# Linear attention with decay feeding an MLP: another layout for the first queries, the key decay moved into v, a mask read with step zero, and another planner

## Chip, cores and metric

The kernel runs on one core of one Trainium2 chip. The metric is device time in microseconds (us) of one execution, as a median over several runs; lower is better. TensorE (PE) multiplies, VectorE (DVE), ScalarE (ACT) and GpSimd (POOL) work elementwise, SyncE (SP) only issues DMAs.

## The reference

Attention with a per-head decay `lam` over blocks of 64 tokens (4 batches, 8 heads, 768 tokens, head size 64), and then an MLP whose activation is h + sin(alpha h)^2 / alpha.

```python
def _attn_ref(q, k, v, lam):
    Dmask = np.where(rel >= 0, lam[:, None, None] ** rel[None], 0.0)
    for b in range(nb):
        intra = np.einsum('bhic,bhjc->bhij', qb, kb) * Dmask[None]
        intra = np.einsum('bhij,bhjd->bhid', intra, vb)
        inter = np.einsum('bhid,bhde->bhie', qb * lam_pow[None], kv_state)
        out[:, :, sl] = intra + inter
        kv_state = lam_block * kv_state + np.einsum('bhsd,bhse->bhde', kb * rev_pow[None], vb)

def _moe_ref(x, w_in, w_out, alpha):          # x: 3072 x 512
    h = x @ w_in                              # 512 x 2048
    s = np.sin(alpha * h)
    return (h + s * s / (alpha + 1e-09)) @ w_out
```

The block size does not change the result; the kernel works in blocks of 128 tokens.

## The kernel before

**Attention.** There are 24 blocks of 128 tokens (6 for each batch), numbered `s`. The decay lam^(i-j) is split into lam^i on the query side and lam^-j on the key side, so that no pair needs its own factor: `Lq` and `Lk` hold the powers, made by iota, a multiply by ln(lam) (`lnL`, DVE), and two exponentials (ACT). For each block, `scale_block` multiplies q by Lq (L464, POOL, two instructions for a pair of blocks) and k by Lk (L471, DVE for blocks 0 and 1, else POOL) into `qk2`, and casts v to bf16 (L473, ACT, or POOL for late blocks). q is loaded for two blocks at once, with two neighbouring tokens on a partition, so that a row of a transfer has 512 bytes; rows of k and v have 256 bytes. `piece_Q` and `piece_T` transpose q and k on PE (L506, L488) and copy them to `qkT` (L511, L493); from block 12 on a DMA transpose does it (L479, on SP's queue). `part_S` multiplies keys by queries into two PSUM banks (L543), and DVE multiplies 128 x 1024 values by `mask` into `Sm` (L552). `part_Z` adds k^T v to the running state in PSUM (L568) and copies it (`Zc`, `Zd`). `part_O` multiplies the state by q (L616, L603) and v by Sm (L623) and copies the output to `xT`, which is the transposed input of the MLP (L632).

**MLP.** Tokens go in six chunks of 512. An A unit makes 128 hidden features of a chunk: four matmuls of 512 columns (L671), a sine (ACT L681), a square (POOL L686 or ACT L685) and h + u/alpha on DVE (L688) into `gT`. `unit_A2` does the same for two feature groups on half a chunk (L705, L715, L719 or L720, L723), so that a chunk can start before all its tokens are there; it serves chunk 1 and the beginnings of chunks 0 and 2. A B unit adds four products with w2 (L736) into a bank for the output; after the fourth, ACT copies it (L749) and a DMA stores it.

**Weights.** The first quarter of w1 comes through SP into `ws` and is cast by DVE (L391). The other three quarters and the four of w2 come through POOL's queue, which casts on the way.

**Order.** Every operation is recorded with an engine (or a choice of engines with durations), its reads and its writes. `_Plan` then plays the program with these durations and appends, one at a time, the operation that can start first; within a margin PE and SP take the one recorded first (less `lead`). SP keeps the order recorded, PE may look 40 operations ahead, ACT, DVE and POOL take what is ready. The order found is the order of each engine's queue, and each wait becomes a semaphore. `_transfers` estimates when loads land, and the planner is run again with that.

**Filler.** While PE has nothing to do before the first A unit, the planner puts `spin` into the holes: matmuls of 512 columns whose result is not used (L829). `P.filler` names what they read.

Of the kernel before, what the change touches and what calls it, by code (L numbers as in the profile page):

```python
# [13 lines left out]
class _Op:  # L14


    def __init__(self, eng, emit, dur, reads, writes, dma, after, issue, lat, runs=64):
        self.eng, self.emit, self.dur = eng, emit, dur
        self.given = eng
        self.issue, self.lat, self.runs = issue, lat, runs  # L20
        self.lead = 0
        self.reads, self.writes, self.dma = reads, writes, dma
        self.port = False
        self.after = after
        self.deps = set()
        self.needed = False
        self.count = None
        self.start = None
        self.done = None
        self.knows = None  # L30


class _Plan:

    AHEAD = {"PE": 40, "SP": 1}
    SLACK = 0.3  # L40
    EARLY = 0.0, 0.0

    LAT = 0.2
# [10 lines left out]
    def op(self, eng, emit, dur, reads=(), writes=(), dma=None, after=(), issue=0.4, lat=2.6, runs=64):  # L54
# [14 lines left out]
        o.deps.discard(o)  # L69
        o.lead = self.lead  # L70
# [4 lines left out]
    def _transfers(order):  # L75
# [5 lines left out]
        left = {e: [[o.start + 0.8, o.runs, o.dur / o.runs, o] for o in sorted(q, key=lambda o: o.start)]  # L81
# [19 lines left out]
    def _settle(self):  # L101

        filler, lands, best = self.filler, {}, None
        for _ in range(8):
            self.filler = filler
            for o in self.ops:
                o.eng, o.start, o.done = o.given, None, None
            order = self._order(lands)
            new = self._transfers(order)
            off = sum(abs(t - o.done) for o, t in new.items())  # L110
            state = [(o, o.eng, o.start, o.done) for o in order]
            if best is None or off < best[0]:
                best = off, order, state
            lands = new
# [4 lines left out]
    def _order(self, lands):  # L119
        index = {o: i - o.lead for i, o in enumerate(self.ops)}  # L120
        left = {}
        for o in self.ops:
            left.setdefault(o.eng if isinstance(o.eng, str) else "any", []).append(o)
        fixed = {e: left.pop(e, []) for e in ("PE", "SP")}
        free = [o for e in left for o in left[e]]
        clock = {e: 0.8 for e in ("PE", "SP", "ACT", "DVE", "POOL")}
        wire = 0.0
        port = 0.0
        order = []

        def ready(o):
            t = 0.0
            for d in o.deps:
                if d.done is None:
                    return None
                t = max(t, d.done + (0.0 if d.eng == o.eng else self.LAT))
            return t

        while fixed["PE"] or fixed["SP"] or free:
            best = None  # L140
            for e in ("PE", "SP"):
                can = []
                for o in fixed[e][:self.AHEAD[e]]:
                    r = ready(o)
                    if r is not None:
                        can.append((max(r, clock[e]), index[o], o, e, o.dur))
                if can:
                    soon = min(c[0] for c in can)
                    soon += self.EARLY[1] if e == "PE" and soon < self.EARLY[0] else self.SLACK
                    c = min((c for c in can if c[0] <= soon), key=lambda c: c[1])  # L150
                    if best is None or c[:2] < best[:2]:
                        best = c
            for o in free:
                r = ready(o)
                if r is None:
                    continue
                if o.port:
                    r = max(r, port)
                if isinstance(o.eng, str):
                    c = (max(r, clock[o.eng]), index[o], o, o.eng, o.dur)  # L160
                else:
                    _, e, d = min((max(r, clock[e]) + d + late, e, d) for e, d, late in o.eng)
                    c = (max(r, clock[e]), index[o], o, e, d)
                if best is None or c[:2] < best[:2]:
                    best = c
            t, _, o, e, dur = best
            if e == "PE" and self.filler is not None:
                emit, reads, last = self.filler
                if last.start is not None:
                    self.filler = None  # L170
                else:
                    deps = [self.writer[b] for b in reads]
                    at = max([clock["PE"]] + [d.done + self.LAT if d.done is not None else t for d in deps])
                    n = int((t - at) / 0.4)
                    if n > 0:
                        f = _Op("PE", lambda h, n=n: emit(h, n), 0.4 * n, tuple(reads), (), None, (), 0, 0)
                        f.deps = set(deps)
                        f.start, f.done = at, at + 0.4 * n
                        order.append(f)
            if isinstance(o.eng, str):  # L180
                (fixed[e] if e in fixed else free).remove(o)
            else:
                free.remove(o)
                o.eng = e
            o.start = t
            if o.dma is not None:
                clock[e] = t + o.issue
                wire = max(wire, t + 0.8) + dur
                o.done = max(t + 0.8 + o.dur + o.lat, lands[o]) if o in lands else wire + o.lat
            else:  # L190
                clock[e] = o.done = t + dur
                if o.port and e != "ACT":
                    port = o.done
            order.append(o)
        return order
# [48 lines left out]
def bass_lightning_attn__then__act_snake_kernel(  # L244
# [14 lines left out]
    BL = 128  # L259
# [17 lines left out]
    RU = 4  # L277

    es = contextlib.ExitStack()
    with es:  # L280
# [18 lines left out]
        q32 = ring("q32", RL // 2, [128, H, 2, D], F32)  # L299
# [8 lines left out]
        mask = sb("mask", [128, 8, 128], BF16)  # L308
        maskf = sb("maskf", [128, 128], F32)
# [4 lines left out]
        E_i = sb("E_i", [128, 2 * NB, H], I32)  # L314
        E_f = sb("E_f", [128, 2 * NB, H], F32)
        lnL = sb("lnL", [128, 2 * NB, H], F32)
        Lq = sb("Lq", [128, NB, H], F32)
# [12 lines left out]
        def _(_unused_eng):  # L330
# [5 lines left out]
            P.EARLY = 20.0, 0.3  # L336
# [4 lines left out]
            def load(dst, src, key, dur, sem, eng="SP", lat=2.6, after=(), issue=0.4, runs=64):  # L341
# [3 lines left out]
            def load_q(s, after=()):  # L345
# [3 lines left out]
                for lo, hi in ((0, 4), (4, H)) if s < 4 else ((0, H),):  # L349
                    last["q32", s] = load(  # L350
                        q32[j][:, lo:hi, :, :].rearrange("p h t d -> p h (t d)"),
                        q[b, lo:hi, n * BL:(n + 2) * BL, :].rearrange("h (p t) d -> p h (t d)", t=2),
                        [("q32", j, a) for a in range(lo // 4, hi // 4)],
                        (0.9 if s == 0 else 1.1 if s < 4 else 2.3), f"q32{j}" + (str(lo) if s < 4 else ""),
                        lat=2.7, after=after, runs=8 * (hi - lo),
                    )

            def load_kv(s, which="kv"):
                b, n, j = s // NB, s % NB, s % RL
                for nm, src, dst in (("k32", k, k32), ("v32", v, v32)):  # L360
                    if nm[0] in which:
# [3 lines left out]
                            (nm, j), 1.1, f"{nm}{j}", lat=2.7,  # L365
# [7 lines left out]
            def load_w1(i, after):  # L373
# [3 lines left out]
                    [("w1", 2 * i), ("w1", 2 * i + 1)], 2.55, f"w1{i}", "POOL", 3.8, after, 0.8, 32,  # L377
                )

            def load_w1_first():  # L380
                for lo in (0, 256):
# [3 lines left out]
                        ("ws", lo), 1.65, f"ws{lo}", lat=2.7, runs=32,  # L385
# [8 lines left out]
            def load_w2(i, after):  # L394
# [3 lines left out]
                    [("w2", 2 * i), ("w2", 2 * i + 1)], 2.55, f"w2{i}", "POOL", 3.8, after, 0.8, 32,  # L398
# [3 lines left out]
            load(lam_bc[:, :], bass.AP(lam.tensor, 0, [[0, 128], [1, H]]), "lam", 0.1, "lam", "ACT", runs=1)  # L402
# [527 lines left out]
```

## Time and profile before

| what | value |
|---|---|
| median of 3 runs | 222.93 us (222.86 to 223.31) |
| profiled execution | 223.52 us, of which the span of the trace is 221.4 |
| PE busy | 208.6 us, 94% of the span, 1645 matmuls |
| ACT, DVE, POOL busy | 155.9, 122.6, 89.1 us |
| first matmul of the MLP | 19.89 us |
| HBM read, written | 27.28 MB, 6.29 MB |
| under 512 bytes | 63520 of 83651 DMA packets |

Times in the trace count from the start of the span. Busy time of PE is the time in which a matmul is in flight, the pipelined overlap counted once. A line number such as L543 is that of the kernel before. A wait is put down to the engine and line whose semaphore came last.

### The profile page before, as it was taken

To read this page: it belongs to the slowest core of one execution; us is meant where nothing else is said; L and a number is where in the kernel's file an instruction comes from. 1 tells how busy PE (TensorE), PEld (TensorE's weight loads), DVE (VectorE), ACT (ScalarE), POOL (GpSimd) and SP (SyncE) were. 2 spreads that over 40 slices of the span, in tenths; PEclk is the share of its full clock that TensorE was granted. 3 is DMA by queue.
4 is the path that set the end of the run, shared out by engine and by line. 5 is a ranking of instruction groups with operands and counts; after the bars stand their busy time and mean duration, and the time that the engine had idled before them with its cause. 6 is when DMAs were issued, how large, how long until landed. Compare 5 with 4: busy or idle time off the path is not lost.

```text
span 221.4 us, 4062 instructions
## 1 busy us (share of the span) xinstructions
PE 208.6 (94%) x1645; PEld 110.7 (50%) x1645; DVE 122.6 (55%) x184; ACT 155.9 (70%) x277; POOL 89.1 (40%) x100
## 2 busy tenths in 40 slices
PE   3889987899898999999999999999999999999995
PEld 1446433456575785545445444545545444444444
DVE  4687775354777887667655455645465544445100
ACT  3735994347697997788788887877788677778211
POOL 4386763454978776863576103011001011110100
DMA  5999999999999999999999752110110011101112
GB/s 131 236 232 271 206 214 208 217 235 237 233 245 275 242 191 245 219 254 189 276 240 245 155 112 33 47 50 0 47 50 21 26 47 50 47 0 49 75 70 95
DMA packets 83651, 33.31 MB, mean 150 GB/s; under 512 B 63520, under 2 KB 80688, under 8 KB 83632
## 3 DMA queue, kind: packets, MB, share of 16 engines
q1 hardware_dynamic: 76880, 24.25, 53.6%
q0 software_dynamic: 3696, 3.67, 9.9%
q10 hardware_dynamic: 3056, 5.13, 6.4%
q8 instruction: 13, 0.21, 0.4%
q14 instruction: 6, 0.05, 0.1%
HBM read 27.28 MB, written 6.29 MB: 152 GB/s over the span
## 4 chain that ended last, share of the span: by engine, by line
PE 63%; DMA 24%; POOL 4%; SPq 4%; ACT 2%; DVE 1%; issue 1%
PE bank L736 32%; PE bank L671 24%; DMA k<-in_k_dram 10%; DMA q<-in_q_dram 5%; DMA v<-in_v_dram 4%; DMA w<-in_moe_w_in_dram 4%; SPq L342 4%; PE bank L705 3%; PE bank L623 2%; PE bank L543 2%; POOL qk L471 1%; POOL qk L464 1%; PE bank L603 1%; POOL u L720 1%; DVE gT L723 1%
## 5 line engine op out<-in xcount | busy, mean ns | idle before, releaser
L736 PE MATMUL bank<-w,gT 128*128 128x512 bf16 (+1 forms) x400 | 94.8, 371 | 0.0
L688 DVE SCALAR_TENSOR_TENSOR gT<-u,rinv,bank 128x512 bf16<-128x512 bf16 x74 | 54.6, 746 | 51.7 <-ACT u L685 34.2
L671 PE MATMUL bank<-xT,w 128*128 128x512 bf16 x296 | 74.2, 379 | 0.6 <-DVE gT L688 0.6
L681 ACT ACTIVATE t<-bank,alpha 128x512 bf16<-128x512 f32 x74 | 50.6, 686 | 24.1 <-PE bank L671 24.0
L736 PEld LDWEIGHTS bank<-w,gT 128*128 128x128 bf16 x400 | 37.7, 98 | 39.6
L686 POOL TENSOR_TENSOR u<-t 128x512 bf16<-128x512 bf16 x19 | 19.7, 1040 | 80.7 <-ACT t L681 79.7
L671 PEld LDWEIGHTS bank<-xT,w 128*128 128x128 bf16 x296 | 28.5, 98 | 34.9 <-DVE gT L688 1.1
L685 ACT ACTIVATE u<-t 128x512 bf16<-128x512 bf16 x55 | 34.4, 629 | 1.8 <-DVE gT L723 0.3
L552 DVE TENSOR_TENSOR Sm<-bank,mask 128x1024 bf16<-128x1024 f32 x24 | 29.2, 1222 | 10.3 <-PE bank L568 7.7
L464 POOL TENSOR_TENSOR qk<-q,Lq 128x512 bf16<-128x512 f32 x24 | 24.5, 1044 | 21.7 <-DMA q<-in_q_dram 18.1
L471 POOL TENSOR_TENSOR qk<-k,Lk 128x512 bf16<-128x512 f32 x22 | 22.9, 1044 | 7.2 <-DMA k<-in_k_dram 7.0
L749 ACT COPY osb<-bank 128x512 f32<-128x512 f32 (+1 forms) x25 | 14.2, 569 | 14.8 <-PE bank L736 14.8
L705 PE MATMUL bank<-xT,w 128*128 128x256 bf16 x176 | 22.3, 273 | 2.0 <-DVE gT L723 2.0
L723 DVE SCALAR_TENSOR_TENSOR gT<-u,rinv,bank 128x256 bf16<-128x256 bf16 x44 | 19.1, 476 | 7.2 <-POOL u L720 4.1
L715 ACT ACTIVATE t<-bank,alpha 128x256 bf16<-128x256 f32 x44 | 18.5, 471 | 3.3 <-PE bank L705 3.1
L705 PEld LDWEIGHTS bank<-xT,w 128*128 128x128 bf16 x176 | 16.2, 98 | 5.5 <-DVE gT L723 3.0
L473 ACT CAST v<-v 128x512 bf16<-128x512 f32 x18 | 11.0, 615 | 7.6 <-DMA v<-in_v_dram 7.6
L632 ACT CAST xT<-bank 128x512 bf16<-128x512 f32 (+1 forms) x18 | 12.9, 716 | 2.8 <-PE bank L568 1.6
L720 POOL TENSOR_TENSOR u<-t 128x512 bf16<-128x512 bf16 x11 | 11.3, 1039 | 4.7 <-ACT t L715 4.6
L543 PE MATMUL bank<-qkT 64*128 64x128 bf16 x192 | 9.8, 226 | 0.2 <-DVE qkT L493 0.2
L623 PE MATMUL bank<-Sm,v 128*64 128x128 bf16 x192 | 9.9, 225 | 0.0
L829 PE MATMUL bank<-mask,ident 128*128 128x512 bf16 x12 | 5.7, 564 | 3.7 <-DVE mask L429 3.7
(55 smaller groups left out, 111.4 us busy)
## 6 DMA issues: line engine op xcount, KB each, us to landing
k<-in_k_dram SPq DMA_DIRECT2D x24, 256.0 KB, 5.5
v<-in_v_dram SPq DMA_DIRECT2D x24, 256.0 KB, 5.5
q<-in_q_dram SPq DMA_DIRECT2D x10, 512.0 KB, 5.5
out_dram<-osb ACTq DMA_DIRECT2D x19, 256.0 KB, 2.0
w<-in_moe_w_out_dram POOLq DMA_DIRECT2D x4, 512.0 KB, 13.1
w<-in_moe_w_in_dram POOLq DMA_DIRECT2D x3, 512.0 KB, 9.0
q<-in_q_dram SPq DMA_DIRECT2D x4, 256.0 KB, 4.6
ws<-in_moe_w_in_dram SPq DMA_DIRECT2D x2, 512.0 KB, 5.4
```

Source lines behind the costliest of these rows:

```text
L464: lambda e, a=a: e.tensor_tensor(qk2[:, j:j + 2, 4 * a:4 * a + 4, :], q32[jq][:, 4 * a:4 * a + 4, :, :].rearrange("p h t d -> p t h d"), b ...
L471: lambda e: e.tensor_tensor(qk2[:, j, H:2 * H, :], k32[jl][:, :, :], lk, ALU.mult), 0.7 if s in (0,1) else 1.05,
L552: op("DVE", lambda e: e.tensor_tensor(Sm[s % 2][:, :, :], banks[:, 512 * b0:512 * b0 + 1024].rearrange("p (c i) -> p c i", i=128), mask[:, ...
L671: ins = e.matmul(ps[hb][:, c0:c1], w1[:, kc, 128 * m:128 * (m + 1)], xT[x][:, kc, c0:c1], start=(kc == 0 and c0 == lo), stop=(kc == NKC - ...
L681: op("ACT", lambda e: e.activation(t16[ju][:, w], ps[hb][:, w], ACTF.Sin, scale=alpha[:, m:m + 1]), 0.69 * f, [bank(hb), "alpha"], [("t16" ...
L685: lambda e: (e.activation(u16[ju][:, w], t16[ju][:, w], ACTF.Square) if e is nc.scalar else e.tensor_tensor(u16[ju][:, w], t16[ju][:, w], ...
L686: e.tensor_tensor(u16[ju][:, w], t16[ju][:, w], t16[ju][:, w], ALU.mult)), 0,
L688: op("DVE", lambda e: e.scalar_tensor_tensor(out=gT[g][:, m, w], in0=u16[ju][:, w], scalar=rinv[:, m:m + 1], in1=ps[hb][:, w], op0=ALU.mul ...
L705: ins = e.matmul(ps[hb][:, 256 * i:256 * i + 256], w1[:, kc, 128 * (m + i):128 * (m + i + 1)], xT[x][:, kc, lo:lo + 256], start=(kc == 0 a ...
L715: op("ACT", lambda e, i=i: e.activation(t16[ju][:, 256 * i:256 * i + 256], ps[hb][:, 256 * i:256 * i + 256], ACTF.Sin, scale=alpha[:, m + ...
L723: op("DVE", lambda e, i=i: e.scalar_tensor_tensor(out=gT[g][:, m + i, lo:lo + 256], in0=u16[ju][:, 256 * i:256 * i + 256], scalar=rinv[:, ...
L736: ins = e.matmul(ps[ob][:, w], gT[g][:, m, 128 * s4:128 * (s4 + 1)], w2[:, m, w], start=(m == 0), stop=(m == NM - 1),)
```

## The change

Five things are changed.

1. **q of blocks 0 to 3** is loaded by two DMAs, each with four heads, all 512 tokens and four neighbouring tokens on a partition (rows of 1,024 bytes), before any k or v. Their scaling has its own powers (`Lq4`, a third iota and a third exponential) and is split between POOL and DVE. Since a column of the transposed q now stands for every fourth token, `part_S` and `part_O` of these blocks read 32 columns out of each of four tiles of `qkT`, and so need all four, and the mask of these blocks is another one.
2. **The decay of the keys** is multiplied into v (POOL) and k is only cast (ACT, or ACT or POOL from block 12 on). The products k v and S v are the same.
3. **The mask** is kept once for each layout (128 x 128) and read with a step of zero over the eight heads.
4. **The planner** models start-up, hand-over and pipelining of engines and the start of transfers, gives margins to all engines, and takes other durations. Early weight loads on POOL wait for v of block 2 instead of k of block 3, and the first of them is given priority.
5. **The filler** reads `Zd` in place of `mask`, which is no longer wide enough.

```diff
-                for lo, hi in ((0, 4), (4, H)) if s < 4 else ((0, H),):
+                if s < 4:
+                    for a in range(2):
+                        last["q32", s] = load(
+                            q32[:, a, :, :, :].rearrange("p (h x) t d -> p h (x t d)", x=2),
+                            q[0, 4 * a:4 * a + 4, 0:4 * BL, :].rearrange("h (p t) d -> p h (t d)", t=4),
+                            [("q32", a, 0), ("q32", a, 1)], 1.45, f"q32{a}", lat=1.25, after=after, runs=32,
+                        )
+                    return
...
-                ported(op("DVE" if s in (0,1) else "POOL",
-                   lambda e: e.tensor_tensor(qk2[:, j, H:2 * H, :], k32[jl][:, :, :], lk, ALU.mult), ...
-                op((("ACT", 0.62, 0.0), ("POOL", 1.05, 0.3)) if s > 11 else "ACT", ... v2[j] from v32[jl]
+                op((("ACT", 0.62, 0.0), ("POOL", 0.62, 0.3)) if s > 11 else "ACT", ... qk2[:, j, H:2 * H] from k32[jl]
+                ported(op("POOL",
+                   lambda e: e.tensor_tensor(v2[j][:, :, :], v32[jl][:, :, :], lk, ALU.mult), 1.05,
...
-                                qkT[r, jt, 4 + jp, :], qkT[r, jq:jq + 2, jp, u],
+                                qkT[r, jt, 4 + jp, :], qkT[r, jq:jq + nq, jp, u],
...
-                        mask[:, :, :], ALU.mult), 1.25, [bank(b0), bank(b1), "mask"], [("Sm", s % 2)])
+                        bass.AP(mask[s >= 4], 0, [[128, 128], [0, 8], [1, 128]]), ALU.mult), 1.22, ...
...
             piece_Q(0, 4)
+            piece_Q(2, 6)
             piece_T(0, 3)
...
-            piece_Q(2, 4)
...
             for i in range(1, 4):
-                load_w1(i, [last["k32", 3]])
+                P.lead = 400 if i <= 1 else 0
+                load_w1(i, [last["v32", 2]])
...
-                    ins = e.matmul(ps[0][:, :], ident[:, :], mask[:, 0:4, :].rearrange("p a b -> p (a b)"))
+                    ins = e.matmul(ps[0][:, :], ident[:, :], Zd[0][:, :, :].rearrange("p a b -> p (a b)"))
...
-                    P.filler = (spin, ("mask", "ident"), u)
+                    P.filler = (spin, (("Zd", 0, 0), ("Zd", 0, 1), "ident"), u)
```

Of the planner, the new constants, the choice of the next operation, and the lines that place the filler (the last four are as before but for names and the hand-over time):

```diff
-    AHEAD = {"PE": 40, "SP": 1}
-    SLACK = 0.3
-    LAT = 0.2
+    AHEAD = 40
+    WINDOW = {"PE": 0.3, "ACT": 0.1, "DVE": 0.1, "POOL": 0.1}
+    PIPE = {"ACT": 0.11, "DVE": 0.09, "POOL": 0.045, "PE": 0.0}
+    HOP = {"PE": 0.055, "ACT": 0.035, "DVE": 0.035, "POOL": 0.075, "SP": 0.1}
+    DRAIN = 0.085
+    MOVES = ()
...
+                soon = min(x[0] for x in c) + self.WINDOW.get(e, 0.0)
+                x = min((x for x in c if x[0] <= soon), key=lambda x: x[1])
+                if best is None or x[0] < best[0]:
+                    best = x[0], x[2], e, x[3]
...
+                    deps = [self.writer[b] for b in reads]
+                    free = max([clock["PE"]] + [d.done + self.HOP["PE"] if d.done is not None else t for d in deps])
+                    n = int((t - free) / 0.4)
+                    if n > 0:
```

More of the change, by code (lines that the diff above doesn't have):

```diff
@@ L52, in __init__, with op @@
         self.lead = 0
-    def op(self, eng, emit, dur, reads=(), writes=(), dma=None, after=(), issue=0.4, lat=2.6, runs=64):
+    def op(self, eng, emit, dur, reads=(), writes=(), dma=None, after=(), issue=0.55, lat=1.4, runs=64, lag=None):
         o = _Op(eng, emit, dur, tuple(reads), tuple(writes), dma, after, issue, lat, runs)
@@ L69, in op @@
         o.deps.discard(o)
+        if lag is not None:
+            o.lag = lag
         o.lead = self.lead
@@ L101, in _settle @@
     def _settle(self):
[L103 to L111, printed above, removed]
+        prio = {o: i - o.lead for i, o in enumerate(self.ops)}
+        for at, width, kind, by in self.MOVES:
+            for o in self.ops[at:at + width]:
+                if kind == "all" or o.given == kind or (kind == "any" and not isinstance(o.given, str)):
+                    prio[o] += by
+        lands, best = {}, None
+        for _ in range(10):
+            order, new, off = self._pass(prio, lands)
             if best is None or off < best[0]:
-                best = off, order, state
+                best = off, order, [(o, o.eng, o.start, o.done) for o in order]
+            if off < 0.5:
+                break
             lands = new
@@ L117, in _settle, with _pass @@
         return best[1]
[L119 to L121 removed]
+    def _pass(self, prio, lands):
         for o in self.ops:
[L123 to L168 removed]
@@ L194, in _order @@
             order.append(o)
+            can.discard(o)
+            left -= 1
+            for s in after.get(o, ()):
+                waits[s] -= 1
+                if not waits[s]:
+                    can.add(s)
         return order
```

253 lines of the change are left out of this document (161 added, 92 removed).

## Prediction

> **What bounds the kernel now.** I read the page first: share by engine, then the 40 slices.
>
> ```profile
> PE 208.6 (94%) x1645; PEld 110.7 (50%) x1645; DVE 122.6 (55%) x184; ACT 155.9 (70%) x277; POOL 89.1 (40%) x100
> ...
> PE   3889987899898999999999999999999999999995
> ...
> DMA  5999999999999999999999752110110011101112
> ```
>
> TensorE is busy 208.6 of 221.4 us; what can be won is its idle 12.8 us plus busy work that is no work. The DMA engines are full from the second slice to the 22nd (5 to 122 us). Next, busy time by stretch (us, then PE, PEld, DVE, ACT, POOL, granted clock, DMA share, GB/s):
>
> ```profile
> 0.00:10.00 10.00, 5.82 (x24) 2.41 (x25) 5.50 (x11) 5.41 (x8) 4.28 (x13) 1.00 0.84 173
> 30.00:40.00 10.00, 7.77 (x39) 3.50 (x40) 5.33 (x8) 5.68 (x9) 4.90 (x5) 1.00 1.20 210
> 120.00:140.00 20.00, 20.00 (x129) 9.50 (x128) 10.65 (x14) 16.11 (x28) 4.93 (x6) 1.00 0.53 113
> ```
>
> From about 87 us to the tail PE stands still for only 0.07 us, so nothing there can be won. The holes are before the first MLP matmul (19.89 us) and between 30 and 86 us. The list of PE's waits (us in total, times, longest) names them:
>
> ```profile
> PE bank L506 <- POOL qk L464: 2.1, 2, 1.7
> PE bank L705 <- DVE gT L723: 2.0, 3, 1.0
> PE bank L488 <- POOL qk L471: 0.7, 2, 0.5
> PE bank L671 <- DVE gT L688: 0.6, 1, 0.6
> ```
>
> After 19.89 us these leave 1.72 us (37.6 to 39.3, the transpose of q of block 4, whose load is late), 0.18 us (block 4's k), 0.57 us, and 2.0 us in the stretch where xT chunk 1 goes through 256-column units. Last, the timeline of the opening (start, us, engine, line):
>
> ```profile
> 3.66 2.74 PE L829 MATMUL bank<-mask,ident 128*128 128x512 bf16 x6 [3.66 <-DVE mask L429]
> ...
> 8.58 0.61 PE L506 MATMUL bank<-ident,qk 128*128 128x128 bf16 x4
> ...
> 11.76 0.61 PE L829 MATMUL bank<-mask,ident 128*128 128x512 bf16 x1
> ...
> 12.31 0.41 PE L623 MATMUL bank<-Sm,v 128*64 128x128 bf16 x8
> 12.68 0.40 PE L506 MATMUL bank<-ident,qk 128*128 128x128 bf16 x4
> ...
> 19.89 1.92 PE L705 MATMUL bank<-xT,w 128*128 128x256 bf16 x16
> ```
>
> The granted clock stands at 1.00 in every stretch, yet four transposes take 0.61 us at 8.58 and 0.40 us at 12.68, and a 512-column filler 0.61 us at 11.76 and 0.38 us at 15.13: PE ran at about half rate until some 12.2 us. So the clock column hides the slow start; the durations show it.
>
> **The change, part by part.**
>
> *The filler.* The twelve L829 matmuls are gone from the changed program (1,633 matmuls for 1,645). The filler now reads Zd, and the planner looks up the last writer of Zd in the whole program; that one has no end time yet, so no free room is ever found. Their 5.7 us of PE time lay in holes: no gain. Whether full rate still comes in time is the first rival below.
>
> *Loads of the opening.* q of blocks 0 to 3 becomes two loads of 512 KB in 1,024-byte rows for four of 256 KB in 512-byte rows. By landings (issue plus us to landing) the second q pair lands at 11.5 and 12.5 after v at 10.6, so 1.9 us for 512 KB, 3.8 for all. The row for 512 KB in 1,024-byte rows is ws: the pair lands by 19.65, v before it at 17.1, so 2.55 us. So 1.25 us less, and since all q now goes first, k0 to v1 land about 0.8 later (k0 at 8.0) and k2, k3, v2, v3 and ws about 1.1 earlier (v3 at 16.2, ws at 17.6 and 18.6). Bounds: 0 to 2 us less. The Trainium skill's "DMA: Bandwidth & Descriptors" (Specifications) has line rate from 512 bytes a row, which would make the saving 0; the rows of q and ws here disagree. By that rule the loads stand at their old times and the sum below would be some 0.3 us poorer.
>
> *Opening, walked.* lnL now stands behind alpha (landed 5.4) and aeps on DVE: Lq at 6.8 for 6.4 before. The q scaling is two rounds of 1.04 (POOL, with DVE at 0.96 beside it): 6.8 to 8.9. S of block 0 now needs all four q blocks: five groups of four transposes at half rate (0.45 each, in line on PE) and the 0.69 q copy bring it to 11.5, with k through an ACT cast (0.62) behind the third table load. Then DVE decides: four Sm at 1.2, one k copy 0.42, Zc 0.43, xT 0.73, w1 cast 0.68 = 7.1, from 12.15, plus 0.4 of hops: 19.7. POOL now scales v (1.04), with the first w1 issue (0.81) queued in front of v2: v3 is ready at 18.0, ahead of O of block 3 (19.0). So the first MLP matmul comes at 19.7 for 19.89: **-0.2** (bounds -1.2, the loads' gain, to +1.0, every PE step of the walk 0.15 slower).
>
> *Weights and q of block 4.* w1's second load waits on v2 (15.0) for k3 (14.9, but issued only at 15.9): each weight load, and the q4 load that waits for w1's third, stands about 1.0 to 1.2 earlier: q4 lands at 37.0 for 38.2. Also the new order puts four more B matmuls and one A unit (0.86 + 0.86) ahead of the q4 transpose. PE gets there at 39.2, q4's halves are scaled by 38.1 and 39.1: the 1.72 us wait goes, and block 4's 0.18 too: **-1.9** (bounds -1.9 to -0.6). Next late would be w2's third part, at 37.4 before PE's use at 40.5, so it hides. The 0.57 us wait on gT stays: ACT needs as much there as before.
>
> *A new hole.* S of block 5 now follows its k transpose directly; before, four B matmuls lay between. The k copy queues on DVE behind Sm of block 4 (1.22): 1.2 + 0.43 against 1.1 us of PE work: **+0.6** (0 to 0.9).
>
> *256-column stretch (52 to 87 us).* Squares move from POOL to ACT: 15 for 11 here. Counting ACT's instructions by their start-to-start times (half sine 0.37, square 0.54, cast 0.52, xT 0.58, Zc 0.27): 31.6 us for 30.3 before. PE has 33.5 of work before, 31.8 after (eight B matmuls have moved ahead). So ACT and PE are level, where ACT had 3 us to spare; before, the stretch took 2.0 more than PE's work. I take the same 2.0: **0** (bounds -2.0 to +2.0). k of a block lands about 1.2 us before v, so ACT's in-line wait (1.69 us on v at 57.16) shrinks; POOL's v scaling waits instead, and little is queued behind it.
>
> *Later.* All squares on ACT from chunk 2 on: 26 us of ACT to 32.5 of PE per chunk: 0. S of block 12 needs DMA transposes that landed at 85.4 for use at 87.25; with loads 1.1 earlier a lead up to some 3 us is not stopped. The mask's zero step (1,222 ns an Sm, float PSUM on the other side): 0, bounds -0.1 to +0.1 each, and only in the opening on the path. k and v trade multiplies for casts one for one: 0.
>
> Sum: -0.2 - 1.9 + 0.6 + 0 = -1.5. The profiled execution took 223.52 us (221.4 span and 2.1 around it), 0.59 above the median of 222.93; both fall by 1.5, so **221.4**. All bounds at once are unlikely; added as squares they give -2.3 and +2.7 about the sum, and half of that, a usual error, makes this case's own range 220.2 to 222.8.
>
> **Rivals.**
>
> *Slower: PE still at half rate when the MLP starts.* In the old run it took from 3.66 to 12.3 us, 8.65 us with holes, or 3.7 us counted from the dense part at 8.58. If the sparser opening (my walk has it about three quarters busy) does not bring full rate, the A units start at half rate for 3.7 to 8.65 us and lose 1.85 to 4.3 of PE time, on the path, since A units follow each other. Middle 3.1: 222.93 - 1.5 + 3.1 = 224.5; from 3.0 us at half rate on, the kernel is slower than before. For: no filler. Against: from 8.85 to 12.6 the walk is as dense as the old 8.58 to 12.3. "TensorE: Matmul & The Clock Gate" of the Trainium skill (Part 4) has transposes not counting as activity, which speaks against this change: full rate would then come only one window (Part 1: about 3.4 us) into the A units, 1.7 us lost, 223.1. That transposes themselves never run at full rate, as it also says, the trace contradicts (0.40 for 0.61); whether they count no row shows.
>
> *The lead runs into ACT.* Level at 31.6 to 31.8, an ACT queue in program order may take 3.5 us over its work, as any k cast waiting for its load stops the sines behind it: the 1.5 us are lost, 222.9.
>
> *All stalls go.* The order planned with better times may also clear the 0.57, the 0.6 and the 2.0: 222.93 - 1.5 - 0.6 - 0.6 - 2.0 = 218.2.
>
> **How the numbers follow.** Forecast 0.45, half rate 0.30, ACT 0.18, all stalls 0.07. Within 0.2% (0.45 us), about what a measurement of this kernel can tell from no change: 0.03 of the first case, 0.02 of the second, 0.07 of the third, 0.12 in all. Faster: 0.41 + 0.03 + 0.05 + 0.07 = 0.56. Slower: 0.01 + 0.25 + 0.06 = 0.32. Range 219.2 to 224.8: the low end leaves out most of the last case, the high end the longer half of the half-rate spans.
>
> **What would show it.** Right: no wait of the q transpose after 30 us; first 256-column A group at 19.7 ± 0.7 and its 16 matmuls in 1.9 us; ws landing near 18.6; a wait of S near 46 us; gT waits near 2 us. Wrong: 16 matmuls in 3.5 us (half rate), first A group after 20.7 (opening), gT waits above 4 us with ACT without idle (ACT bound), or any wait after 90 us.

## The result, and the profile after

| | before | after |
|---|---|---|
| median | 223.31 us (222.62 to 224.82, 17 runs) | 225.33 us (223.57 to 227.18, 17 runs) |
| profiled execution | 223.52, span 221.4 | 224.99, span 222.8 |

The ratio is 1.0077, 95% interval 1.0053 to 1.0100: slower by 0.8%, where 221.4 was forecast. Ratios leave out runs more than 1.5% above the fastest of their kernel (here 226.97 and 227.18 us) and are made on one chip at a time, so they are not the quotients of the medians. The kernel before lies between 223.1 and 223.9 from session to session, so kernels of different sessions are compared by ratios.

First the page of the changed kernel: spans, shares by engine, the 40 slices.

```profile
span 222.8 us, 4045 instructions
...
PE 207.8 (93%) x1633; PEld 112.4 (50%) x1633; DVE 120.1 (54%) x179; ACT 168.0 (75%) x305; POOL 70.5 (32%) x82
...
PE   0489999999999998999999999999999999999995
```

ACT has 12 us more work and POOL 19 less, as the squares moved. PE's weak place is now the first three slices alone. Busy time by stretch, with the columns that the prediction names (time, then PE, PEld, DVE, ACT, POOL, granted clock, DMA share, GB/s):

```profile
0.00:10.00 10.00, 1.26 (x10) 0.93 (x11) 4.87 (x12) 5.33 (x10) 5.16 (x15) 1.00 0.79 188
30.00:40.00 10.00, 9.47 (x45) 4.09 (x44) 7.36 (x11) 9.11 (x16) 6.89 (x7) 1.00 1.19 209
120.00:140.00 20.00, 20.00 (x148) 9.73 (x143) 10.57 (x14) 17.64 (x32) 4.74 (x5) 1.00 0.75 137
```

From 30 to 40 us PE gained 1.7 us (7.77 to 9.47). In the first 10 us it works 1.26 us for 5.82: the filler is gone. PE's waits of 0.5 us and more are these (us in total, times, longest):

```profile
PE bank L475 <- DMA alphaT<-in_moe_alpha_dram: 6.2, 1, 6.2
PE bank L547 <- DVE qk L496: 2.5, 2, 1.7
PE bank L754 <- DVE xT L681: 0.8, 1, 0.8
PE bank L672 <- DVE Sm L600: 0.5, 1, 0.5
PE bank L720 <- DVE gT L737: 0.5, 1, 0.5
PE bank L591 <- DVE qkT L534: 0.5, 1, 0.5
```

After the opening there is no wait for q of block 4 and none for gT in the 256-column stretch; 0.83 us for xT at 87 us and 0.52 us at S of block 5 are new. Last, PE's timeline (start, us, engine, line):

```profile
10.42 0.63 PE L529 MATMUL bank<-ident,qk 128*128 128x128 bf16 x4
...
21.10 0.64 PE L672 MATMUL bank<-Sm,v 128*64 128x128 bf16 x8
21.67 3.57 PE L754 MATMUL bank<-xT,w 128*128 128x256 bf16 x16
25.06 1.91 PE L720 MATMUL bank<-xT,w 128*128 128x512 bf16 x8
...
42.53 0.39 PE L547 MATMUL bank<-ident,qk 128*128 128x128 bf16 x4
```

The pieces that took 0.41 us before take 0.64 up to 21.7 us, and the sixteen first MLP matmuls 3.57 for 1.92: PE is at half rate until 25 us (the granted clock stands at 1.00 all this time). Against the kernel before, the first MLP matmul comes 1.78 us later, and half rate behind it costs 1.65. Then follow -1.72 and -0.18 (block 4), +0.52 (S of block 5), -2.0 (gT), +0.83 (xT) and +0.23 (osb, at 98.75). That is +1.1 of the +1.4 us between the spans. The loss sits in the first 25 us, and 2.3 us of it are won back.

### The profile page after: what moved, and what is told of

The parts are those of the page before. It is cut to its first block, busy times and chain, and to the rows that moved or that the text cites. A ratio compares the mean times of both kernels' runs of the same rounds, so it can differ in the third digit from the quotient of the medians.

```text
span 222.8 us, 4045 instructions
## 1 busy us (share of the span) xinstructions
PE 207.8 (93%) x1633; PEld 112.4 (50%) x1633; DVE 120.1 (54%) x179; ACT 168.0 (75%) x305; POOL 70.5 (32%) x82
## 4 chain that ended last, share of the span: by engine, by line
PE 82%; ACT 7%; DVE 5%; DMA 2%; issue 1%; POOL 0%; ACTq 0%
PE bank L785 36%; PE bank L720 24%; PE bank L754 8%; PE bank L672 4%; PE bank L591 3%; ACT t L730 2%; DMA alphaT<-in_moe_alpha_dram 2%; PE bank L665 2%; DVE Sm L600 2%; ACT u L734 1%; PE bank L547 1%; PE bank L529 1%; ACT t L764 1%; PE bank L652 1%; PE bank L616 1%
## 5 line engine op out<-in xcount | busy, mean ns | idle before, releaser
L720 PEld LDWEIGHTS bank<-xT,w 128*128 128x128 bf16 x296 | 28.8, 98 | 35.2 <-DVE gT L737 1.3
L734 ACT ACTIVATE u<-t 128x512 bf16<-128x512 bf16 x69 | 43.4, 629 | 2.1
L514 POOL TENSOR_TENSOR v<-v,Lk 128x512 bf16<-128x512 f32 x24 | 24.9, 1043 | 18.3 <-DMA v<-in_v_dram 14.6
L754 PE MATMUL bank<-xT,w 128*128 128x256 bf16 x176 | 24.1, 286 | 1.0 <-DVE xT L681 0.8
L506 POOL TENSOR_TENSOR qk<-q,Lq 128x512 bf16<-128x512 f32 x20 | 20.4, 1042 | 9.1 <-DMA q<-in_q_dram 9.0
L764 ACT ACTIVATE t<-bank,alpha 128x256 bf16<-128x256 f32 x44 | 18.6, 475 | 5.7 <-PE bank L754 5.7
L754 PEld LDWEIGHTS bank<-xT,w 128*128 128x128 bf16 x176 | 16.7, 102 | 5.5 <-DVE gT L772 1.5
L681 ACT CAST xT<-bank 128x512 bf16<-128x512 f32 (+1 forms) x18 | 14.1, 789 | 1.4 <-PE bank L672 1.4
L511 ACT CAST qk<-k 128x512 bf16<-128x512 f32 x19 | 11.6, 623 | 0.6 <-DMA k<-in_k_dram 0.5
L672 PE MATMUL bank<-Sm,v 128*64 128x128 bf16 x192 | 10.8, 240 | 0.5 <-DVE Sm L600 0.5
L769 POOL TENSOR_TENSOR u<-t 128x512 bf16<-128x512 bf16 x6 | 6.2, 1038 | 14.5 <-ACT t L764 14.5
L768 ACT ACTIVATE u<-t 128x512 bf16<-128x512 bf16 x16 | 10.2, 639 | 0.3
L591 PEld LDWEIGHTS bank<-qkT 64*128 64x128 bf16 x192 | 6.0, 100 | 5.7 <-issue 1.7
```

Source lines behind the costliest of these rows:

```text
L506: lambda e, a=a: e.tensor_tensor(qk2[:, j:j + 2, 4 * a:4 * a + 4, :], q32[:, jq, 4 * a:4 * a + 4, :, :].rearrange("p h t d -> p t h d"), b ...
L514: lambda e: e.tensor_tensor(v2[j][:, :, :], v32[jl][:, :, :], lk, ALU.mult), 1.05,
L591: ins = e.matmul(ps[(b0, b1)[h]][:, 128 * jp:128 * (jp + 1)].rearrange("p (t x) -> p t x", t=nq), qkT[r, jt, 4 + jp, :], qkT[r, jq:jq + nq ...
L672: ins = e.matmul(ps[obs[jp // 2]][64 * h:64 * h + 64, 128 * jp:128 * (jp + 1)], v2[j][:, 2 * jp + h, :], Sm[s % 2][:, 4 * h + jp, :], star ...
L720: ins = e.matmul(ps[hb][:, c0:c1], w1[:, kc, 128 * m:128 * (m + 1)], xT[x][:, kc, c0:c1], start=(kc == 0 and c0 == lo), stop=(kc == NKC - ...
L734: lambda e: (e.activation(u16[ju][:, w], t16[ju][:, w], ACTF.Square) if e is nc.scalar else e.tensor_tensor(u16[ju][:, w], t16[ju][:, w], ...
```

## Experiments

**1. The filler.** Theory A: its absence is the loss. Theory B: the loss is the opening's work on DVE and POOL.

```diff
- P.filler = (spin, (("Zd", 0, 0), ("Zd", 0, 1), "ident"), u)
+ P.filler = (spin, (("Zd0", 0), "ident"), u)   # "Zd0": written by the memset alone
```

> The changed kernel, with the filler's dependence written so that the planner finds the memset of Zd and not the last writer of Zd in the program; all else as in the changed kernel. Theory A (the missing filler is the loss: TensorE runs the O pieces in 0.64 us for 0.41, the first MLP matmuls in 3.57 for 1.9 and the first second-layer units of the pair late): the sixteen matmuls of the first stretch take about 1.9 us again, the first MLP matmul starts at about 21 instead of 21.67, and the time falls by 2 to 3 us, to 222.5 to 223.5, level with the kernel before or just under it. Theory B (the opening's own work on VectorE and GpSimd is the loss, and TensorE's rate follows from real work alone): the filler changes less than 0.7 us; 224.6 to 225.5.

Measured: 223.17 us (222.25 to 227.16, 12 runs), ratio 1.0003 (0.9972 to 1.0035). Its timeline:

```profile
13.91 0.61 PE L880 MATMUL bank<-Zd,ident 128*128 128x512 bf16 x1
14.52 0.41 PE L672 MATMUL bank<-Sm,v 128*64 128x128 bf16 x8
...
20.77 2.02 PE L754 MATMUL bank<-xT,w 128*128 128x256 bf16 x16
22.62 1.89 PE L720 MATMUL bank<-xT,w 128*128 128x512 bf16 x8
```

Full rate comes at 14.5 us, the first MLP matmul 0.9 earlier, the sixteen in 2.02 us, the first 512-column unit 2.44 us earlier. The median falls by 2.2 us; by the ratios (1.0077 and 1.0003) it is 0.74%, or 1.7 us. By the ratios that is over B's 0.7 and a little under A's 2 to 3; the full rate in the trace decides for A. The first MLP matmul still comes 0.9 us later than before: that part is B's.

The reverse, the kernel before without its filler (`P.filler` left out):

> The kernel before, with its twelve filler matmuls taken out and nothing else changed. Theory A: the opening of the kernel before gets the long pieces too, the sixteen first MLP matmuls take 3.5 us, and the time rises by 1.5 to 3 us, to 224.5 to 226. Theory B: the attention work of blocks 0 to 3 brings TensorE up by itself; within 0.5 us of the kernel before (223.3).

Measured: 223.84 us (223.16 to 224.69, 12 runs), ratio 1.0022 (1.0001 to 1.0044). A's expectation missed and B's came: by the ratio the kernel is 0.5 us slower, and the sixteen matmuls took 1.92 us.

```profile
15.91 0.72 PE L488 MATMUL bank<-ident,qk 128*128 128x128 bf16 x8
17.08 0.62 PE L543 MATMUL bank<-qkT 64*128 64x128 bf16 x16 [0.45 <-ACT qkT L493]
...
20.62 1.92 PE L705 MATMUL bank<-xT,w 128*128 128x256 bf16 x16
```

Without a filler the old opening still reaches full rate at some 16.5 us, and pays 0.73 us at the first MLP matmul. So a filler has no fixed worth: when full rate comes without one changes from run to run, as profiled runs of the changed kernel show below (16 us in one, 25 to 28 in the others). The time with a filler is not fixed either: full rate came at 12.3 us in the profile of the kernel before and at 7.7 in that of its variant with a later S (experiment 4).

**2. The copy into xT**, which took 1.30 us for 0.73 with four tokens on a partition. Walked in the order of xT's columns (filler mended):

```diff
- ..."p a (x t) -> p a t x"... , ..."p (a t x) -> p a t x"...
+ ..."p a (x t) -> p a x t"... , ..."p (a t x) -> p a x t"...
```

> The changed kernel with the filler mended as above, and the copy of the attention output into xT walked in the order of xT's own columns, so that it writes contiguously and reads PSUM with steps. If the step of the write is what makes the copy of a four-token block cost 1.30 us on VectorE where the two-token block's cost 0.73: the copy falls to 0.6 to 0.8 us, the opening is up to 0.6 us shorter and the time 0 to 0.6 us under that of the changed kernel with the filler mended alone. If the step costs the same on the read side: the copy stays at 1.2 to 1.4 us and the time within 0.3 us.

Measured: 223.94 us (222.64 to 226.51, 12 runs), ratio 1.0015 (0.9984 to 1.0047). DVE's timeline, with the filler mended alone and then with the other walk:

```profile
16.45 1.31 DVE L681 CAST xT<-bank 128x512 bf16<-128x512 f32 x1 [0.19 <-PE bank L672]
```

```profile
16.43 0.69 DVE L681 CAST xT<-bank 128x512 bf16<-128x512 f32 x1 [0.19 <-PE bank L672]
```

The copy falls to 0.69 us and the first MLP matmul comes at 20.28 for 20.77; the time shows nothing of it within its interval, as the runs are spread over 3.9 us.

**3. Planner and features apart.** A further question is what the planner and the other changes do alone. The new planner (filler mended) with the old q loads, decay in k and v cast:

> The new planner with its new costs, and the filler mended, on the old features: q of blocks 0 to 3 with two tokens on a partition in four loads, the decay multiplied into k, v cast on ScalarE; of the features only the mask's step of zero is there. If the planner alone brings the 3.9 us that the changed kernel wins back after its first MLP matmul (the waits for q4 and for gT): the time is 220.5 to 221.8, under both kernels, with no gT waits between 120 and 140 us. If the features (decay in v, which frees ScalarE, and the larger q loads) bring them: the gT waits stay, and the time is 222.5 to 224.

Measured: 226.60 us (224.81 to 229.11, 6 runs), ratio 1.0117 (1.0071 to 1.0162). Both expectations missed. Its trace stands 2.31 us at S of block 12 in front of the DMA transpose, and the granted clock behind that is low; the profiled run with the filler mended (its slowest, 227.16) has the same two things:

```profile
PE bank L591 <- DMA qkT<-qk: 3.1, 1, 3.1
```

```profile
90.00:100.00 10.00, 10.00 (x64) 4.77 (x63) 5.75 (x9) 7.89 (x15) 5.26 (x6) 0.85 1.21 234
```

The columns of the second are those of the stretches above. 3.1 us of standing and 15% of the next 10 us make 4.6, and this run lies 4.5 us above 222.7, the middle of the kernel's seven fastest runs. That gave theory C (the standing in front of the transpose, and the low clock behind it, spread the runs), tried by moving S of blocks 12 and 13 later (SP's order is unchanged):

```diff
- if block <= NBLK and m in ((2, 6, 8, 11, 13) if c == 2 else (2, 7, 10, 13)):
+ if block <= NBLK and m in ((5, 7, 9, 11, 13) if c == 2 else (2, 7, 10, 13)):
      # prep(block + 2) stays at m = 2, 6, 8, 11, 13
```

> The changed kernel with the filler mended, and S of blocks 12 and 13 put some 5 and 2 us later in TensorE's order (behind A units 5 and 7 of chunk 2 for 2 and 6; SyncE's order is the same). Theory C (in the mended kernel what spreads the runs from 222.3 to 227.2 is S of block 12 standing in front of its DMA transpose, by a length that varies from run to run, and a long stand of that kind is followed by some 10 us at a granted clock of 0.85): all runs fall between 222.0 and 223.4, median 222.4 to 222.9, no wait on qkT in the trace. Theory D (the runs spread by how long TensorE stays at half rate in the opening): the spread stays, with a second group of runs near 224.5.

Measured: 222.16 us (221.77 to 223.96, 12 runs), ratio 0.9973 (0.9940 to 1.0006); no wait on qkT. The runs above 224 are gone, as C has it, but a second group stays, four runs from 223.7 to 224.0 beside eight from 221.8 to 222.4. C explains the top only, and against the mended kernel (1.0003) the gain of 0.3% lies within the intervals.

The old q loads with the rest of the mended kernel:

> The changed kernel with the filler mended, and q of blocks 0 to 3 back at two tokens on a partition in four loads in the old order of loads; the decay stays in v. If the four-token q costs (q scaled in 1.11 and 1.51 us, all four blocks before the first S, the copy into xT 1.30 us for 0.73): the first MLP matmul comes at 20.0 to 20.3 for 20.77 and the time is 0.3 to 0.8 under the mended kernel. If the layout is what makes the mended kernel better than the new planner with the old features (226.6): 225 to 227, with the half-rate or DMA waits of that run.

Measured: 223.39 us (222.56 to 224.61, 12 runs), ratio 1.0006 (0.9979 to 1.0032), first MLP matmul at 20.48, and 1.5 us of waiting on qkT. Against the mended kernel (1.0003) the four-token layout shows neither gain nor loss by itself. What separates this kernel from the new planner with all the old features (1.0117) is the place of the decay.

The new features under the old planner:

> The new features (q of blocks 0 to 3 with four tokens on a partition, the decay multiplied into v, the mask's step of zero, the squares and copies at the new choices of engine) under the old planner with its old constants, with the filler working. The new planner with the old features gave 226.6, with the new ones 223.2. If the features gain by themselves what separates those two (3.4 us) and the new planner costs 3.4: 219.8 to 221. If the features only undo a harm that the new planner's order does to the old features: 222.5 to 223.5. If the old planner's order does not suit the new features: above 224.

Measured: 228.28 us (227.81 to 229.05, 6 runs), ratio 1.0220 (1.0172 to 1.0268), with 3.9 us in front of S of block 12. The features alone do not gain; decay in v and the new planner go together.

All mends at once, with alphaT expected later by the planner (2.8 for 2.0), which puts lnL ahead of alpha and aeps on DVE:

> All mends together: the filler, the copy into xT in xT's order, S of blocks 12 and 13 later, and a longer time for alphaT in the planner, so that lnL stands before alpha and aeps on VectorE (q scaling from 6.5 for 7.3). Theory C and the opening's walk together: the first MLP matmul at 19.4 to 19.9, no wait on qkT, 221.2 to 222.0, below both kernels. If an earlier TensorE only meets the DMA transposes of the next blocks: 222.3 to 223.0 with waits on qkT after 90 us.

Measured: 222.91 us (221.58 to 223.60, 12 runs), ratio 0.9972 (0.9944 to 1.0001). Neither expectation holds: the time is that of the second, but there is no wait on qkT. In its trace the first MLP matmul comes at 21.85, because lam landed at 6.9 us where other traces have 4.4. That became theory F in experiment 5: the small first loads land late in some runs.

**4. The later S as a control.** S of blocks 12 and 13 is put later in four more kernels: the changed kernel, the kernel before, and the planner and the features alone (in these two S is also made to wait for A units 5 and 7). The changed kernel first.

> The changed kernel as it is (no filler runs), with S of blocks 12 and 13 later as in the mended kernel. If the two losses (no filler in the opening, S of block 12 in front of its transpose) stand side by side: TensorE comes to 87 us some 2.4 us later than in the mended kernel, so that the transpose mostly lands in time and little is left to win there: 224.0 to 225.2, but no run above 226. If the stand at block 12 is what makes the changed kernel slow and the filler is a small thing: 222.2 to 223.2.

Measured: 224.90 us (222.87 to 227.14, 12 runs) beside 223.85 for the kernel before, ratio 1.0022 (0.9982 to 1.0062). The median is as the first theory has it, the runs above 226 stay: they hold something else.

> The kernel before with the same two pieces later. Its trace has no wait at the DMA transposes, S of block 12 comes at 87.25 with its transpose landed at 85.4. If the later place only helps an order that is ahead of its transfers: within 0.4 us of the kernel before (223.1). If S of block 12 stands in some runs of the kernel before too (its runs go from 221.8 to 225.2): 0.4 to 1 us faster, with the runs above 224 gone.

Measured: 223.22 us (222.70 to 225.26, 12 runs) beside 223.85 for the kernel before, ratio 0.9971 (0.9940 to 1.0001). If the later place helps, it helps the kernel before as much as the mended one (0.3% in both, and in both within the intervals). So a gain there would not be a cost of the change.

> The new planner with the old features (226.6), with S of blocks 12 and 13 held behind A units 5 and 7. If its loss is the stand of 2.3 us and the low clock behind it (0.76 and 0.80 from 84 to 100 us, some 4 us in all): 222.4 to 223.6, level with the kernel before, and then the planner by itself gains or loses nothing. If the order of the planner with the old features is slow by itself: above 225.

Measured: 226.37 us (224.45 to 228.29, 12 runs), ratio 1.0102 (1.0069 to 1.0134). No wait on qkT in its trace, which was its fastest run, yet nothing gained: why the new planner with the old features is slow is open.

> The new features under the old planner (228.3), with S of blocks 12 and 13 held behind A units 5 and 7. Its trace stands 3.9 us at S of block 12, with a clock of 0.77 and 0.79 from 84 to 100 us. If the features by themselves gain, and the stand hid it: 221.5 to 222.5. If the old planner's order costs them what the trace shows before 84 us (first MLP matmul in two parts with 0.95 between, gT 1.1): 223.5 to 225.

Measured: 228.26 us (227.65 to 230.07, 6 runs), ratio 1.0208 (1.0155 to 1.0261). The stand is gone and 4.1 and 2.4 us of waits on gT have come in its place, in a profile of its slowest run.

**5. What the changed kernel's runs above 226 us hold.** Three single profiled runs of the changed kernel, as it is. E is half rate, C the standing at block 12, F the late first loads. The expectations of the three were alike; that of the first:

> The changed kernel unchanged, one profiled run. Half rate (E): a run above 226 has the first second-layer units (512-column, eight matmuls from 25.06 on) in over 2.5 us too, and no wait on qkT. Stand at block 12 (C): a run above 226 has a wait on qkT of 1.5 us or more and a granted clock under 0.9 from 90 to 100 us. Late first loads (F): lam lands at 6 us for 3.9 and the first MLP matmul comes at 23 or later for 21.67. A run near 225 has none of these and repeats the first profile.

Measured: 227.37, 227.22 and 226.56 us. In all three lam is late. The DMA view of the first two microseconds, in the profile of 224.99 and then in the first of the three (packets by queue, q10 carries ACT's loads and q1 SP's; issues with us to landing):

```profile
q10 hardware_dynamic: 9, 0.00, 0.2%
q1 hardware_dynamic: 1, 0.00, 0.1%
...
q<-in_q_dram SPq DMA_DIRECT2D x2, 512.0 KB, 5.6
...
lam_bc<-in_lam_dram ACTq DMA_DIRECT2D x1, 4.0 KB, 3.9
alphaT<-in_moe_alpha_dram ACTq DMA_DIRECT2D x1, 8.0 KB, 4.8
```

```profile
q1 hardware_dynamic: 9, 0.01, 1.5%
...
q<-in_q_dram SPq DMA_DIRECT2D x2, 512.0 KB, 7.5
...
lam_bc<-in_lam_dram ACTq DMA_DIRECT2D x1, 4.0 KB, 6.2
alphaT<-in_moe_alpha_dram ACTq DMA_DIRECT2D x1, 8.0 KB, 7.0
```

Where nearly all the first packets are ACT's, lam lands after 3.9 us; where they are q's, after 6.2, and everything behind is 2.2 us later. PE's timeline of the same run:

```profile
8.42 0.25 PE L475 MATMUL bank<-identf,alphaT 16*128 16x16 f32 x1 [8.42 <-DMA alphaT<-in_moe_alpha_dram]
...
23.85 3.60 PE L754 MATMUL bank<-xT,w 128*128 128x256 bf16 x16
27.24 2.19 PE L720 MATMUL bank<-xT,w 128*128 128x512 bf16 x8
```

227.37 - 224.99 = 2.4 us. F explains the first two times, and neither E nor C does: the first run is 2.2 us behind the profile of 224.99 at the first MLP matmul, 2.5 behind the first 512-column unit, and still 2.5 at the last matmul. F explains the third only in part. It had full rate at 16.2 us and its first MLP matmul at 22.42, 0.75 behind, but then a granted clock of 0.83 from 20 to 30 us, so that the sixteen matmuls took 3.57 us again; the other 0.8 of its 1.6 us come after 87 us, with a wait of 0.6 on gT among them.

A second profiled run of the kernel with all mends:

> The kernel with all mends (filler, copy into xT in xT's order, S of blocks 12 and 13 later, lnL first), one more profiled run. If late first loads are chance: lam lands at 3.5 to 3.9, the first MLP matmul comes at 19.4 to 20.2 for 21.85, and the time is 221.5 to 222.2. If the changed order of VectorE's instructions brings them: lam at 6.1 again, and 222.9 again.

Measured: 226.04 us, lam after 6.0 again, so the time missed both expectations. The first profiled run of this kernel (223.06 us) had lam as late and its first MLP matmul at 21.85, this one at 21.75. The 3.0 us between the two come later, 1.4 of them as waits on gT after 85 us: late loads are not all that spreads the runs. Twelve profiles have two 512 KB loads of q at the head and lam on ACT's queue: in seven q's packets are first and lam lands after 6.0 to 6.2 us, in five ACT's are first and it lands after 3.5 to 3.9. Six have loads of 256 KB: in four of these q's packets are first too, and lam lands after 3.8 to 3.9 all the same (3.7 in the other two). The four single runs of this experiment came from one chip and were all late; whether the chip has a part in it is open. In these profiles it takes both, q first and the larger loads. To try it, the two small loads were put in front on SP's queue, all else in place:

```diff
- order = self._settle()
+ order = sorted(self._settle(), key=lambda o: o.dma not in ("lam", "alphaT"))
+ for o in order[:2]: o.eng = "SP"
```

> The changed kernel with one thing moved: the two small loads (lam and alphaT) stand at the head of SyncE's queue, before the two 512 KB loads of q, for a queue of their own on ScalarE; every other instruction stays in its place. Theory F (lam and alphaT land at 4.7 and 6.1 us in some runs and at 7.0 and 8.3 in others, as the packets of q come second or first on the DMA engines, and this spreads the changed kernel's runs by 2.1 us): lam lands by 4 us in every run, q some 0.5 to 1 us later; the runs above 226 are gone, median 224.0 to 225.0, half rate at the first MLP units as before. If the late first loads come from the start of the DMA engines as a whole, whoever is first in the queue: the runs above 226 stay, median 225 to 226.

Measured: 223.73 us (223.26 to 225.89, 12 runs), ratio 1.0007 (0.9976 to 1.0037), no run above 226, and the median under the 224.0 to 225.0 expected. With no filler the loss is gone:

```profile
lam_bc<-in_lam_dram SPq DMA_DIRECT2D x1, 4.0 KB, 2.6
alphaT<-in_moe_alpha_dram SPq DMA_DIRECT2D x1, 8.0 KB, 2.3
```

```profile
11.03 1.28 PE L591 MATMUL bank<-qkT 64*128 64x128 bf16 x16
...
20.93 2.69 PE L754 MATMUL bank<-xT,w 128*128 128x256 bf16 x16
23.46 1.89 PE L720 MATMUL bank<-xT,w 128*128 128x512 bf16 x8
```

The first S comes at 11.03 for 12.27, and PE is still at half rate up to some 22 us. Against the profile of 224.99 the first MLP matmul comes 0.74 us earlier, and the sixteen matmuls take 0.88 less. These 1.6 us stay to the end.

> The kernel with all mends (filler, copy into xT in xT's order, S of blocks 12 and 13 later, lnL before alpha and aeps), with lam and alphaT at the head of SyncE's queue in the same way. Theory F: first MLP matmul at 19.7 to 20.7 for 21.75 and 21.85, no run above 223.2, median 221.3 to 222.0, under both kernels. If the start of the DMA engines is slow whoever is first: as the kernel with all mends, 222.9 (221.6 to 223.6).

Measured: 223.99 us (222.44 to 228.16, 12 runs), ratio 0.9975 (0.9946 to 1.0003): missed. lam landed in time, the first MLP matmul came at 20.16, but this run took the gain back in another way:

```profile
10.00:20.00 10.00, 7.97 (x132) 5.14 (x129) 8.31 (x10) 5.00 (x10) 6.06 (x7) 0.96 1.26 253
20.00:30.00 10.00, 10.00 (x61) 5.30 (x56) 5.87 (x11) 8.02 (x16) 6.72 (x8) 0.87 1.22 199
```

PE was at full rate from 12.6 us, and at 19.1 us the granted clock fell for some 4 us, so that the sixteen matmuls took 3.13 us. Seven of the twelve runs lie from 223.9 to 224.3, beside four from 222.4 to 222.8, so the two groups stay with lam in time.

The filler alone (1.0003) and the move alone (1.0007) each take the whole loss away within their intervals, and all mends with the move (0.9975) bring no more than filler and later S did (0.9973). So the gains of filler and move do not add up. No version is shown to beat the kernel before: the three lowest ratios, 0.9972, 0.9973 and 0.9975, have intervals that reach 1.0001 to 1.0006.

## Why the prediction was wrong, point by point

**The filler at no cost: wrong.** That the holes it filled were free was right as far as it went (1,633 matmuls, as told). But its work also decided when PE reaches full rate. The rival of that name had 0.30 and 224.5 us; its mechanism happened. The filler put back brought 2.44 us in the traces, 2.2 by the medians and 1.7 by the ratios, which is the low end of its 1.85 to 4.3. The case against it, that the walk was as dense from 8.85 to 12.6 us as the old one, failed since full rate does not follow a density at a fixed time: the changed program reached it at 16.2 us in one run and at 25 to 28 us in others. What settles it in a run is open. The Trainium skill's "TensorE: Matmul & The Clock Gate" (Part 1) says that the window is free-running, and that the number of slow matmuls changes from run to run; these runs agree, with a spread of some 10 us. Its Part 4, that transposes do not count in the same way, would, as the prediction read it, put full rate one window (3.4 us) behind the first A unit, at 25.1: the profile of 224.99 has 25.06, the run with 16.2 us speaks against it as a rule.

**Loads of the opening, 1.25 us less: wrong; they saved nothing.** ws landed at 18.5 and 20.0 us, for 18.7 and 20.1 before and 17.6 and 18.6 forecast. The prediction took the pair of before to land by 19.65; with 20.1 its own row gives some 0.9 us less, not 1.25. And that row did not carry over to q: the first 512 KB landed at 5.9 us, as the first two loads of 256 KB did before, the second took 1.6 us more for 1.85, and v of block 3 landed at 17.1 for 17.2. "DMA: Bandwidth & Descriptors" (Specifications) of the Trainium skill, line rate from 512 bytes a row, has the saving at 0, and the trace agrees within 0.2 us. What the two large loads did instead was no term at all: ahead of lam and alphaT, they made these late by 2.1 to 2.3 us in some of the runs. Moving the two brought the ratio from 1.0077 to 1.0007. That it is q's packets in front that make them late fits the twelve profiles and the move, though the move changes both the order and the queue; why q's come first in some runs only is not known.

**The opening's walk, -0.2: wrong by 1.1 us even with the filler** (20.77 to 20.91 for 19.7). alphaT landed at 6.1 for 5.4, and lnL behind it gave Lq at 7.14 for 6.8. Scaling on both engines at once took 1.51 us on POOL and 1.11 on DVE, for 1.04 and 0.96: the two rounds were 3.0 us for 2.1. The copy into xT was 1.30 for 0.73, by the step of its write. That is 0.9 to 1.0 later than before, at the end of the bounds, and half rate put some 0.8 on top.

**Weights and q of block 4, -1.9: right.** The q transposes at 42.53 wait for nothing; the 0.57 us on gT stayed (0.53). The reason given was half right, and the rest was luck: q of block 4 landed 0.4 us earlier, not 1.1, since POOL issued its second weight load only at 19.2 us, for 16.9 before, behind its scaling of v. PE was later and had more work ahead. With the first MLP matmul at 20.28 (experiment 2), 0.75 us of this wait were back.

**The new hole at S of block 5, +0.6: right,** 0.52 us at 50.66.

**The 256-column stretch, 0 (-2.0 to +2.0): inside the bounds at -1.2, but the waits were wrong.** ACT and PE were level, as told (60 to 70 us: ACT busy all 10.0), yet all 2.0 us of gT waits went, and 0.83 for xT came.

**Later, 0: right in the changed kernel** (0.23 us). That a lead of some 3 us would not be stopped at block 12 was wrong: with the filler mended, PE came there at 85.95 us, a lead of 1.3 on the kernel before, and in one run it stood 3.1 us, as the transpose landed at 89.0 for 85.3, and paid a low clock on top.

So the range (219.2 to 224.8) was passed by 0.5 us: 221.4 plus 2.2 for half rate, 1.1 for the walk and, in some of the runs, 2.2 for the late small loads, less the gain of about 1 us in the 256-column stretch, gives 223.7 to 225.9. The profile of 224.99, with lam in time, belongs at the low end and lies 1.3 above it. Of this, 0.6 is that the profile of before lay that much over its median; the other 0.7 is half rate and walk being larger in that run and what the spans leave unexplained.

## What to carry to other kernels

Work that is no work can still set the rate of what follows: before a warm-up or filler is dropped or its dependence renamed, look for it in the order of instructions, and price it at the first real matmuls. Small loads that a whole chain waits for are safer ahead of the large ones on the same queue than beside them on another, as here. Where runs of one kernel spread more than those of the other, profile several before explaining the median.

## What was not expected of the hardware

- The first packets of two queues that start together come in either order, in runs of the same program: beside two loads of 512 KB lam landed after 3.5 to 3.9 us or after 6.0 to 6.2, beside loads of 256 KB after 3.7 to 3.9 either way, and after 2.6 in front on one queue.
- A granted clock below 1.00, right behind a stand of PE (0.85 over 10 us after 3.1 us; none after 1.5 us in another run) or at the first dense matmuls (0.83 and 0.87 from 20 to 30 us); half rate at the start does not show in that column at all.
- A copy of 128x512 values from PSUM to bf16 takes 1.30 us where its write steps by four elements, 0.73 by two, 0.69 with the step on the read side.
- Two multiplies at once on POOL and DVE (q times Lq) took 1.51 and 1.11 us on average; the shortest on DVE was 0.69.
